# One level of Strassen's scheme in the second product of an attention and feed-forward kernel

## The chip, the cores and the metric

The kernel runs on one core of one Trainium2 chip. The metric is the device time of one execution in microseconds; the kernel before takes 854.92 us (median of three runs, 854.73 to 856.07). One further execution was taken by the hardware profiler, and every line of a profile below comes from such an execution. The engines are TensorE (PE in the profile; PEld is its loading of the stationary operand), VectorE (DVE), ScalarE (ACT), GpSimd (POOL) and SyncE (SP), which issues most of the DMAs.

## The reference

```python
# x: (8, 8, 512, 64)   state: (8, 8, 32, 64)   (batch, head, rows, D)
scores = x @ state.T / sqrt(D);  a  = softmax(scores);  xread = a  @ state
scores2 = state @ x.T / sqrt(D); a2 = softmax(scores2); sread = a2 @ x
attn = concatenate([xread, sread], axis=2)          # (8, 8, 544, 64)
t = attn.transpose(0, 2, 1, 3).reshape(8 * 544, 512)
h = t @ w_in                                         # w_in (512, 2048)
sp = maximum(h, 0) + log1p(exp(-abs(h)))             # softplus
g = h * erf(sp)
out = g @ w_out                                      # w_out (2048, 512)
```

x and state are f32. Both weights come as 64-bit floats, and the kernel turns them into f32 on the chip. All matmuls are f32.

## The kernel before, in words

There are nine chunks of rows: the 512 x rows of each of the eight batches, and one state chunk with the 8 × 32 = 256 state rows of all batches. Each chunk goes through a first product (rows by 512 times 512 by 2048), an elementwise step and a second product (rows by 2048 times 2048 by 512). The 2048 features are walked in four groups `g` of 512, so of four tiles of 128.

For a batch the first product is folded with the attention read: `mixed` (L229 to L232) multiplies the states with `w_in` into a tile `m`, two 128-row halves for each batch and group, and `hidden` multiplies that with the transposed softmax `aT`, so a tile of h needs two matmul calls. The state chunk takes its rows from `sT` and needs four calls a tile. `attention` (L126 and on) computes the softmax matrices of one batch: transposes into `xT` (L141, L143), scores (L151), softmax (L162 to L181), and in its inner function `rest` the second softmax and the read of x (L186 to L216). The weights are converted by `weight` (L100 to L104) group by group during batch 0.

`hidden` (L244 to L249) makes one group: four tiles `hp` in PSUM (a pool of two banks), each with a Softplus by ScalarE into `s` (L246) and a copy by VectorE into `hs` (L247); then one Erf by ScalarE over the whole of `s` (L248) and one multiplication by VectorE, `s = s * hs` (L249). `project` (L255) multiplies `s` as the stationary operand, 128 rows by 128 features at a time, with 512 columns of `w_out`, and adds up over all groups in one PSUM bank for each 128 rows, four accumulators `o0` to `o3`, with one buffer each. `store` copies them out by ScalarE (L263) and sends them off by SP's queue (L270 for batches, L277 for the state chunk).

The main loop is software-pipelined by one group: the code calls `hidden` of group g, and after it the projection of the group before (`pending`). After that come `mixed` of the next batch, one group in each turn, and once a batch `attention` of the next batch (in turn 3 of batch 0, in turn 1 of the others).

No queue is written out by hand. Inside its tile context the kernel gives each instruction a tile to read or write, and the framework's planner lays out the queue of each engine from the calls; an instruction that comes earlier in the code goes first where both are ready. The order in the trace is therefore not always the order of the calls. An engine then works through its own queue in that order, with semaphore waits on the others.

Of the kernel before, what the change touches and what calls it, by code (L numbers as in the profile page):

```python
# [8 lines left out]
F32 = mybir.dt.float32  # L9
U32 = mybir.dt.uint32  # L10
ALU = mybir.AluOpType
ACTF = mybir.ActivationFunctionType
# [4 lines left out]
def kernel(  # L17
# [23 lines left out]
    T = S + Ns  # L41
# [92 lines left out]
    def attention(b):  # L134
# [22 lines left out]
        a = att.tile([P, 2, NC * NI, Ns], F32, name="a")  # L157
# [25 lines left out]
        def rest():  # L183
            a2 = att.tile([P, 2, S], F32, name="a2")
# [50 lines left out]
    def hidden(pairs, n):  # L235

        hs = act.tile([P, GF, S], F32, name="hs")[:, :, 0:n]
        s = act.tile([P, GF, S], F32, name="s", bufs=3)[:, :, 0:n]  # L240
        for i in range(GF):
            hp = ps_h.tile([P, S], F32, name="h")
            for k, (lhsT, rhs) in enumerate(pairs):
                nc.tensor.matmul(out=hp[:, 0:n], lhsT=lhsT[:, P * i:P * i + P], rhs=rhs,  # L244
                                 start=(k == 0), stop=(k == len(pairs) - 1))
            nc.scalar.activation(out=s[:, i, :], in_=hp[:, 0:n], func=ACTF.Softplus)  # L246
            nc.vector.tensor_copy(hs[:, i, :], hp[:, 0:n])  # L247
        nc.scalar.activation(out=s, in_=s, func=ACTF.Erf)  # L248
        nc.vector.tensor_tensor(s, s, hs, op=ALU.mult)  # L249
        return s  # L250

    def project(gT, n, g, acc):
        for r in range(n // P):
            for i in range(GF):
                nc.tensor.matmul(out=acc[r], lhsT=gT[:, i, P * r:P * r + P],  # L255
                                 rhs=w_out[:, GF * g + i, :],
                                 start=(g == 0 and i == 0),
                                 stop=(g == NG - 1 and i == GF - 1))

    def store(acc, n, put):  # L260
        for r in range(n // P):
            ot = outs.tile([P, d_model], F32, name="ot")
            nc.scalar.copy(ot, acc[r])  # L263
            put(r, ot)

    def put_x(b):
        rows = out[T * b:T * b + S].rearrange("(p c) e -> c p e", c=NC)

        def go(r, ot):
            nc.sync.dma_start(out=rows[r], in_=ot)  # L270
        return go

    def put_s(r, ot):
        m = P // Ns
        for j in range(m):
            r0 = T * (m * r + j) + S
# [12 lines left out]
    pending = None  # L289
    for b, (n, put) in enumerate(chunks):  # L290
        acc = None
        for g in range(NG):
# [9 lines left out]
            gT = hidden(pairs(b, g), n)  # L302
# [47 lines left out]
```

## Time and profile before

| what | value |
|---|---|
| time, median of 3 runs | 854.92 us |
| time of the profiled execution | 856.09 us |
| span of the profiled execution, first to last instruction | 854.3 us |
| mean granted TensorE clock | 0.981 |
| busy TensorE, weight load, VectorE, ScalarE | 827.7, 379.0, 310.8, 388.9 us |
| matmul records of the second product (L255) | 1088 |

One call of `nc.tensor.matmul` on f32 operands appears as two matmul records and two weight-load records. In the views a group of instructions has its line, engine, operation, output and input with their shapes, the count after an x, then the busy time and the mean length of one in nanoseconds, and after a second bar the idle time of that engine just before them with what ended it. Busy times of TensorE are unions: records of neighbouring matmuls overlap, so the mean length of one is more than the spacing from one to the next. A row of the timeline or of the chain of waits has the start, the length, the engine, the line, the operation and how many were merged.

### The profile page before, as it was taken

How to read it: one execution, taken by the hardware profiler on the slowest of the kernel's cores; microseconds unless marked ns; L12 is line 12 of the kernel's file. 1: busy time of each engine (PE TensorE's matmuls, PEld its weight loads, DVE VectorE, ACT ScalarE, POOL GpSimd, SP SyncE). 2: the span in 40 equal slices, each digit the busy share in tenths (PEclk: the TensorE clock that was granted, in tenths of full speed). 3: DMA queues.
4: the chain of work that ended last, by engine and by line, in shares of the span. 5: the costliest groups of instructions: out<-in, count | busy, mean ns of one | idle time of the engine just before them, and what ended most of it. 6: DMA issues, size and time to landing. Idle time of an engine off the chain costs nothing.

```text
span 854.3 us, 7812 instructions
## 1 busy us (share of the span) xinstructions
PE 827.7 (97%) x3216; PEld 379.0 (44%) x3216; DVE 310.8 (36%) x436; ACT 388.9 (46%) x494; POOL 0.7 (0%) x6
## 2 busy tenths in 40 slices
PE   3689999999999999999999999999999999999997
PEld 2233345444444444454444444454444444445564
DVE  2979524452222522262224422262224322222121
ACT  5778535563344534373344534373445434333332
POOL 0000000000000000000000000000000000000000
PEclk7689999999999999999999999999999999999999
DMA  7658102002010200002010201000000001000100
GB/s 251 188 186 263 72 0 82 18 0 51 0 50 0 51 0 38 12 1 50 0 51 0 51 0 50 0 1 1 16 34 0 2 0 50 0 0 1 49 1 25
DMA packets 45474, 35.10 MB, mean 41 GB/s; under 512 B 36992, under 2 KB 36992, under 8 KB 45440
## 3 DMA queue, kind: packets, MB, share of 16 engines
q1 hardware_dynamic: 45056, 34.55, 13.1%
q8 instruction: 25, 0.41, 0.2%
q10 hardware_dynamic: 384, 0.07, 0.0%
q14 instruction: 9, 0.07, 0.0%
HBM read 25.69 MB, written 8.91 MB: 41 GB/s over the span
## 4 chain that ended last, share of the span: by engine, by line
PE 91%; DVE 0%; ACT 0%; issue 0%
PE o L255 53%; PE h L244 28%; PE at L229 4%; PE at L141 1%; PE at L151 1%; PE at L208 1%; PE at L196 1%; PE at L179 1%; PE at L162 1%; PE at L215 0%; PE at L130 0%; DVE m L232 0%; ACT ot L263 0%
## 5 line engine op out<-in xcount | busy, mean ns | idle before, releaser
L255 PE MATMUL o<-w_out,s 128*128 128x512 f32 x1088 | 484.2, 594 | 0.0
L255 PEld LDWEIGHTS o<-w_out,s 128*128 128x128 f32 x1088 | 203.8, 190 | 247.3 <-issue 244.6
L244 PE MATMUL h<-aT,m 128*128 128x512 f32 x512 | 241.8, 608 | 0.9 <-ACT m L231 0.7
L247 DVE COPY hs<-h 128x512 f32<-128x512 f32 (+1 forms) x144 | 94.9, 661 | 246.3 <-ACT s L246 246.2
L246 ACT ACTIVATE s<-h 128x512 f32<-128x512 f32 (+1 forms) x144 | 82.3, 573 | 185.5 <-PE h L244 185.0
L244 PEld LDWEIGHTS h<-aT,m 128*128 128x128 f32 x512 | 93.9, 193 | 125.8 <-issue 117.2
L249 DVE TENSOR_TENSOR s<-s,hs 128x2048 f32<-128x2048 f32 (+1 forms) x36 | 78.3, 2174 | 74.0 <-ACT s L248 74.0
L231 ACT COPY m<-at 128x512 f32<-128x512 f32 x32 | 18.7, 584 | 158.5 <-PE at L229 158.2
L232 DVE COPY m<-at 128x512 f32<-128x512 f32 x32 | 22.1, 690 | 169.7 <-PE at L229 169.7
L248 ACT ACTIVATE s<-s 128x2048 f32<-128x2048 f32 (+1 forms) x36 | 65.4, 1816 | 0.4
L246 ACT ACT_TABLE_LOAD x43 | 55.2, 1283 | 0.8
L263 ACT COPY ot<-o 128x512 f32<-128x512 f32 x34 | 19.7, 580 | 59.9 <-PE o L255 57.9
L248 ACT ACT_TABLE_LOAD x36 | 46.2, 1283 | 0.6
L229 PE MATMUL at<-w_in,stT 64*32 64x512 f32 x512 | 40.6, 628 | 0.4 <-DVE m L232 0.4
L244 PE MATMUL h<-sT,w_in 128*128 128x256 f32 x128 | 28.9, 379 | 0.0
L244 PEld LDWEIGHTS h<-sT,w_in 128*128 128x128 f32 x128 | 24.3, 190 | 6.7 <-issue 3.8
L143 ACT COPY xT<-at 128x512 f32<-128x512 f32 x32 | 17.3, 589 | 7.8 <-PE at L141 7.8
L141 PEld LDWEIGHTS at<-ident,x 128*128 128x128 f32 x128 | 15.9, 148 | 8.8 <-ACT m L231 3.5
L141 PE MATMUL at<-ident,x 128*128 128x128 f32 x128 | 17.9, 286 | 0.9 <-DMA x<-in_x_dram 0.9
L229 PEld LDWEIGHTS at<-w_in,stT 64*32 64x32 f32 x512 | 6.4, 106 | 27.0 <-issue 20.8
L179 PE MATMUL at<-ident,a 128*128 128x128 f32 x64 | 9.4, 292 | 7.7 <-DVE a L173 7.7
L151 PE MATMUL at<-xT,stT 64*32 64x512 f32 x128 | 11.9, 637 | 2.5 <-ACT xT L143 2.5
(50 smaller groups left out, 287.0 us busy)
## 6 DMA issues: line engine op xcount, KB each, us to landing
x<-in_x_dram SPq DMA_DIRECT2D x64, 128.0 KB, 3.3
raw<-in_moe_w_in_dram SPq DMA_DIRECT2D x8, 1024.0 KB, 5.9
hs<-in_moe_w_out_dram SPq DMA_DIRECT2D x8, 1024.0 KB, 5.2
out_dram<-ot SPq DMA_DIRECT2D x32, 256.0 KB, 2.3
out_dram<-ot SPq DMA_DIRECT2D x8, 64.0 KB, 1.7
st<-in_state_dram SPq DMA_DIRECT2D x8, 56.0 KB, 5.5
st<-in_state_dram ACTq DMA_DIRECT2D x8, 8.0 KB, 2.2
```

Source lines behind the costliest of these rows:

```text
L141: nc.tensor.transpose(out=xp[:, P * c:P * c + P], in_=xt[:, c, 2 * i:2 * i + 2, :], identity=ident)
L151: nc.tensor.matmul(out=s2[e][q, :], lhsT=stT[b][r, q], rhs=xT[r, i, :], start=True, stop=True)
L229: nc.tensor.matmul(out=ps[e][q, :], lhsT=stT[b][r, q], rhs=w_in[r, g, i, :], start=True, stop=True)
L231: nc.scalar.copy(mg[:, 0], ps[0])
L232: nc.vector.tensor_copy(mg[:, 1], ps[1])
L244: nc.tensor.matmul(out=hp[:, 0:n], lhsT=lhsT[:, P * i:P * i + P], rhs=rhs, start=(k == 0), stop=(k == len(pairs) - 1))
L246: nc.scalar.activation(out=s[:, i, :], in_=hp[:, 0:n], func=ACTF.Softplus)
L247: nc.vector.tensor_copy(hs[:, i, :], hp[:, 0:n])
L248: nc.scalar.activation(out=s, in_=s, func=ACTF.Erf)
L249: nc.vector.tensor_tensor(s, s, hs, op=ALU.mult)
L255: nc.tensor.matmul(out=acc[r], lhsT=gT[:, i, P * r:P * r + P], rhs=w_out[:, GF * g + i, :], start=(g == 0 and i == 0), stop=(g == NG - 1 a ...
L263: nc.scalar.copy(ot, acc[r])
```

## The change

The second product of batches 1 to 7 and of the state chunk goes by one level of Strassen's algorithm, in the variant with shared sums. It works on parts of 256 rows by 1024 features by 512 columns, each cut in two along all three: A11 to A22 are 128 rows by 512 features, B11 to B22 are 512 features by 256 columns. In place of eight products of such quarters there are seven. Batch 0 keeps the plain product.

The weight combinations T1, T2, T4 are made by three subtractions on VectorE at the end of batch 0 (`combine_w`); T3 overwrites B12 once batch 0's projection has read it (`last`). The combinations S1 to S4 of the activations are made for each part by `combine_g`, called at the head of `project7`, four VectorE operations of 128x512 that write over `hs`. `project7` adds up the seven products in seven half-banks of the four accumulators, over two parts of 1024 features. `store7` adds the half-banks together on VectorE, with one ScalarE copy, and puts out two times 128 rows.

A chunk's turns change with it: for batches 1 to 7 a turn is now 256 rows by 1024 features (two halves of rows, two parts of features each, in the order 0, 1, 1, 0), and the first product streams 256 columns in each matmul, two feature tiles side by side in one `hp` bank. The state chunk has two turns in place of four. `s` has two buffers in place of three, and the attention tiles `a` and `a2` become slices of a tile that takes the buffer of `xT`.

```diff
...
         for e in range(2):
             nc.scalar.copy(sc[:, e], s2[e])
-        a = att.tile([P, 2, NC * NI, Ns], F32, name="a")
+        both = att.tile([P, NI, S], F32, name="xT")
+        a = both[:, 0:2].rearrange("p e (k n) -> p e k n", n=Ns)
         aT[b] = keep.tile([P, 2, S], F32, name="aT")
...
             nc.vector.tensor_copy(aT[b][:, e], ps)
         def rest():
-            a2 = att.tile([P, 2, S], F32, name="a2")
+            a2 = both[:, 2:4]
...
-    def hidden(pairs, n):
-        hs = act.tile([P, GF, S], F32, name="hs")[:, :, 0:n]
-        s = act.tile([P, GF, S], F32, name="s", bufs=3)[:, :, 0:n]
-        for i in range(GF):
+    def hidden(b, fts, t0, n):
+        hs = act.tile([P, 4, S], F32, name="hs")
+        s = act.tile([P, 4, S], F32, name="s")
+        m = S // n
+        for i in range(4):
             hp = ps_h.tile([P, S], F32, name="h")
-            for k, (lhsT, rhs) in enumerate(pairs):
-                nc.tensor.matmul(out=hp[:, 0:n], lhsT=lhsT[:, P * i:P * i + P], rhs=rhs,
-                                 start=(k == 0), stop=(k == len(pairs) - 1))
-            nc.scalar.activation(out=s[:, i, :], in_=hp[:, 0:n], func=ACTF.Softplus)
-            nc.vector.tensor_copy(hs[:, i, :], hp[:, 0:n])
+            for j in range(m):
+                ops = pairs(b, fts[m * i + j], slice(t0, t0 + n))
+                for k, (lhsT, rhs) in enumerate(ops):
+                    nc.tensor.matmul(out=hp[:, n * j:n * j + n], lhsT=lhsT, rhs=rhs,
+                                     start=(k == 0), stop=(k == len(ops) - 1))
+            nc.scalar.activation(out=s[:, i, :], in_=hp, func=ACTF.Softplus)
+            nc.vector.tensor_copy(hs[:, i, :], hp)
         nc.scalar.activation(out=s, in_=s, func=ACTF.Erf)
         nc.vector.tensor_tensor(s, s, hs, op=ALU.mult)
-        return s
-    def project(gT, n, g, acc):
-        for r in range(n // P):
+        return s, hs
+    def project(gT, g, acc):
+        for r in range(NC):
             for i in range(GF):
                 nc.tensor.matmul(out=acc[r], lhsT=gT[:, i, P * r:P * r + P],
                                  rhs=w_out[:, GF * g + i, :],
                                  start=(g == 0 and i == 0),
                                  stop=(g == NG - 1 and i == GF - 1))
...
+    E2 = d_model // 2
+    wb = w_out.rearrange("p (g h i) (c e) -> p g h i c e", h=2, i=GF, c=2)
+    B11, B12, B21, B22 = (wb[:, :, h, :, c, :] for h in range(2) for c in range(2))
+    T = {}
+    def combine_w():
+        T[1], T[2] = (act.tile([P, 2 * GF * P * 2], U32, name="raw", bufs=2).bitcast(F32)
+                      .rearrange("p (g i e) -> p g i e", i=GF, e=E2) for _ in range(2))
+        T[4] = const.tile([P, NG // 2, GF, E2], F32, name="T4")
+        sub = lambda o, x, y: nc.vector.tensor_tensor(o, x, y, op=ALU.subtract)
+        sub(T[1], B12, B11)
+        sub(T[2], B22, T[1])
+        sub(T[4], B21, T[2])
+        def last():
+            sub(B12, B22, B12)
+            T[3] = B12
+        return last
+    def combine_g(gT, hs):
+        gv = gT.rearrange("p (h i2) (i1 r t) -> p h (i2 i1) r t", h=2, i1=2, r=2)
+        S4 = hs.rearrange("p (k i2) (i1 t) -> p k (i2 i1) t", i2=1, i1=GF)
+        A11, A12, A21, A22 = (gv[:, h, :, r, :] for r in range(2) for h in range(2))
+        S1, S2, S3, S4 = (S4[:, k] for k in range(4))
+        tt = nc.vector.tensor_tensor
+        tt(S1, A21, A22, op=ALU.add)
+        tt(S2, S1, A11, op=ALU.subtract)
+        tt(S3, A11, A21, op=ALU.subtract)
+        tt(S4, A12, S2, op=ALU.subtract)
+        return A11, A12, A22, S1, S2, S3, S4
+    def project7(gT, hs, g, first, last, acc):
+        A11, A12, A22, S1, S2, S3, S4 = combine_g(gT, hs)
+        for lhs, rhs, bank, c in ((A11, B11, 2, 0), (A12, B21, 0, 0), (A22, T[4], 1, 0),
+                                  (S2, T[2], 0, 1), (S3, T[3], 2, 1), (S1, T[1], 1, 1),
+                                  (S4, B22, 3, 0)):
+            for i in range(GF):
+                nc.tensor.matmul(out=acc[bank][:, E2 * c:E2 * c + E2], lhsT=lhs[:, i, :],
+                                 rhs=rhs[:, g, i, :], start=(first and i == 0 and c == 0),
+                                 stop=(last and i == GF - 1 and (c == 1 or bank == 3)))
+    def store7(acc, put):
+        twice = lambda t: t.unsqueeze(1).to_broadcast([P, 2, E2])
+        two = lambda t: t.rearrange("p (c e) -> p c e", c=2)
+        m1, u3 = (outs.tile([P, E2], F32, name=n) for n in ("m1", "u3"))
+        o1, o2 = (outs.tile([P, d_model], F32, name="ot") for _ in range(2))
+        c12 = o1[:, E2:]
+        add = lambda o, x, y: nc.vector.tensor_tensor(o, x, y, op=ALU.add)
+        nc.scalar.copy(m1, acc[2][:, 0:E2])
+        add(two(o1), twice(m1), two(acc[0]))
+        add(u3, c12, acc[2][:, E2:])
+        add(two(o2), twice(u3), two(acc[1]))
+        put(1, o2)
+        add(c12, c12, acc[1][:, E2:])
+        add(c12, c12, acc[3][:, 0:E2])
+        put(0, o1)
+    def put_x(b, h):
+        rows = out[TB * b:TB * b + S].rearrange("(p c) e -> c p e", c=NC)
         def go(r, ot):
-            nc.sync.dma_start(out=rows[r], in_=ot)
+            nc.sync.dma_start(out=rows[2 * h + r], in_=ot)
         return go
     def put_s(r, ot):
...
-    def pairs(b, g):
+    def pairs(b, f, toks):
+        g, fs = f // GF, slice(P * (f % GF), P * (f % GF) + P)
         if b < B:
-            mg = m_t.pop((b, g))
-            return [(mg[:, e], aT[b][:, e]) for e in range(2)]
-        return [(w_in[:, g, k, :], sT[:, k].rearrange("p b n -> p (b n)"))
+            return [(m_t[b, g][:, e, fs], aT[b][:, e, toks]) for e in range(2)]
+        return [(w_in[:, g, k, fs], sT[:, k].rearrange("p b n -> p (b n)")[:, toks])
                 for k in range(NK)]
+    def tiles(n):
+        return [ps_o.tile([P, d_model], F32, name="o%d" % r) for r in range(n)]
+    def plain(b):
+        box = []
+        def project_(g, gT):
+            if g == 0:
+                box.extend(tiles(NC))
+            project(gT, g, box)
+            if g == NG - 1:
+                store(box, lambda r, ot: put_x(b, r // 2)(r % 2, ot))
+        for g in range(NG):
+            yield lambda g=g: hidden(b, range(GF * g, GF * g + GF), 0, S)[0], \
+                lambda gT, g=g: project_(g, gT)
+    def fast(b, parts, put):
+        for h in range(parts):
+            box = []
+            def project_(gT, k, g, h, box):
+                if k == 0:
+                    box.extend(tiles(4))
+                project7(*gT, g, k == 0, k == 1, box)
+                if k == 1:
+                    store7(box, put(h))
+            for k in range(2):
+                g = k ^ (h & 1)
+                yield lambda g=g, h=h: hidden(b, range(2 * GF * g, 2 * GF * g + 2 * GF),
+                                              2 * P * h, 2 * P), \
+                    lambda gT, k=k, g=g, h=h, box=box: project_(gT, k, g, h, box)
     states(0)
     rest = attention(0)
-    chunks = [(S, put_x(b)) for b in range(B)] + [(B * Ns, put_s)]
-    pending = None
-    for b, (n, put) in enumerate(chunks):
-        acc = None
-        for g in range(NG):
+    pending = last = None
+    for b in range(B + 1):
+        if b == 0:
+            groups = plain(b)
+        elif b < B:
+            groups = fast(b, 2, lambda h, b=b: put_x(b, h))
+        else:
+            groups = fast(b, 1, lambda h: put_s)
+        for g, (first, second) in enumerate(groups):
             if b == 0:
                 weights_in(g)
                 mixed(0, g)
...
             if b + 1 < B and g == (1 if b == 0 else 0):
                 load_x(b + 1)
                 states(b + 1)
-            gT = hidden(pairs(b, g), n)
+            gT = first()
             if b == 0 and g == 0:
                 rest()
             if pending is not None:
                 pending()
-            if acc is None:
-                acc = [ps_o.tile([P, d_model], F32, name="o%d" % r) for r in range(n // P)]
-            def pending(gT=gT, n=n, g=g, acc=acc, put=put):
-                project(gT, n, g, acc)
-                if g == NG - 1:
-                    store(acc, n, put)
+            if last is not None:
+                last()
+                last = None
+            if b == 0 and g == NG - 1:
+                last = combine_w()
+            def pending(gT=gT, second=second):
+                second(gT)
             if b + 1 < B and (b or g):
                 for i in [g] if b or g > 1 else [0, 1]:
                     mixed(b + 1, i)
```

More of the change, by code (lines that the diff above doesn't have):

```diff
@@ L40 @@
     NG = NF // GF
-    T = S + Ns
+    TB = S + Ns
     scale = 1.0 / (D ** 0.5)
@@ L258, in project, with store @@
                                  stop=(g == NG - 1 and i == GF - 1))
-    def store(acc, n, put):
-        for r in range(n // P):
+    def store(acc, put):
+        for r in range(NC):
             ot = outs.tile([P, d_model], F32, name="ot")
@@ L264, in store @@
             put(r, ot)
-    def put_x(b):
-        rows = out[T * b:T * b + S].rearrange("(p c) e -> c p e", c=NC)
+    E2 = d_model // 2
[14 more added lines that the diff above has]
+        return last
@@ L275, in put_s @@
         for j in range(m):
-            r0 = T * (m * r + j) + S
+            r0 = TB * (m * r + j) + S
             nc.sync.dma_start(out=out[r0:r0 + Ns], in_=ot[Ns * j:Ns * j + Ns, :])
-    def pairs(b, g):
+    def pairs(b, f, toks):
+        g, fs = f // GF, slice(P * (f % GF), P * (f % GF) + P)
         if b < B:
-            mg = m_t.pop((b, g))
-            return [(mg[:, e], aT[b][:, e]) for e in range(2)]
-        return [(w_in[:, g, k, :], sT[:, k].rearrange("p b n -> p (b n)"))
+            return [(m_t[b, g][:, e, fs], aT[b][:, e, toks]) for e in range(2)]
+        return [(w_in[:, g, k, fs], sT[:, k].rearrange("p b n -> p (b n)")[:, toks])
```

## The prediction

> **What bounds the kernel now.** I read the page first: the busy times, then the chain that ended last.
>
> ```profile
> span 854.3 us, 7812 instructions
> PE 827.7 (97%) x3216; PEld 379.0 (44%) x3216; DVE 310.8 (36%) x436; ACT 388.9 (46%) x494; POOL 0.7 (0%) x6
> PE 91%; DVE 0%; ACT 0%; issue 0%
> ```
>
> TensorE's share is 97%, no other engine reaches half, and the chain is 91% TensorE. Next the busy time by stretches (columns: the stretch, its length, then busy time and instructions of PE, PEld, DVE, ACT, POOL, then the granted clock): does that hold where the second product runs?
>
> ```profile
> 0.00:50.00 50.00, 28.54 (x172) 13.14 (x173) 31.62 (x47) 33.39 (x42) 0.70 (x6) 0.73 0.68 200
> 200.00:400.00 200.00, 200.00 (x796) 88.83 (x795) 65.26 (x95) 86.60 (x113) 0.00 (x0) 1.00 0.09 25
> ```
>
> Only the opening has holes. From batch 1 on TensorE is busy all 200.00 us of a 200.00 us stretch, at clock 1.00. So the kernel is paid for in matmul streaming time, and less of it is less time, as long as no new wait appears. Which matmuls? The groups by line, shapes kept apart (one call of nc.tensor.matmul on f32 shows as two records):
>
> ```profile
> L255 PE MATMUL o<-w_out,s 128*128 128x512 f32 x1088 | 484.2, 594 | 0.0
> L244 PE MATMUL h<-aT,m 128*128 128x512 f32 x512 | 241.8, 608 | 0.9 <-ACT m L231 0.7 <-DVE hs L247 0.2
> L255 PEld LDWEIGHTS o<-w_out,s 128*128 128x128 f32 x1088 | 203.8, 190 | 247.3 <-issue 244.6 <-DVE s L249 0.7 <-ACT s L246 0.5
> L244 PEld LDWEIGHTS h<-sT,w_in 128*128 128x128 f32 x128 | 24.3, 190 | 6.7 <-issue 3.8
> ```
>
> The second product (L255) is 484.2 us, over half the span. Its mean of 594 ns is not its price, since neighbours overlap; the price is the spacing within a long run, which the chain of waits shows (columns: start, length, what):
>
> ```profile
> 345.60 1.72 PE o L255 x4
> 347.32 3.43 PE h L244 x8
> 350.75 12.02 PE o L255 x28
> 780.76 3.45 PE h L244 x16
> ```
>
> 28 records of 512 columns in 12.02 us are 0.4293 us each. The last row is the state chunk, whose first product has 256 columns: 16 in 3.45 us, 0.2156 us each. That is the price of the half-width matmul that the change is made of, measured in this kernel, each record with a weight load of its own (190 ns) that fits under 216.
>
> **The change part by part.** The columns streamed. The second product of batches 1 to 7 and of the state chunk is now 7 × 128 + 64 = 960 records of 512 columns: 960 × 0.4293 = 412.1 us. After, each 256 rows by 1024 features take seven products of four calls, 56 records of 256 columns; there are 7 × 2 × 2 + 2 = 30 such steps, so 1680 × 0.2156 = 362.2 us. That is −49.9 us. Batch 0 stays plain. The first product of batches 1 to 7 is split into 256 columns: 7 × 64 = 448 records at 0.4293 (192.3 us) become 896 at 0.2156 (193.2 us), +0.9. On TensorE the sum is −49.0 us.
>
> The first place where a rule speaks against it. Weight loads grow by 720 + 448 = 1168, and at 190 ns they sit 88% full under each 0.2156 us matmul. In the state chunk 16 of them in a row did not lengthen the spacing, so I charge nothing. The Trainium skill, "TensorE: Matmul & The Clock Gate", Part 3, The mechanism, says that a weight load overlaps a running matmul only where its row group differs, and these all use the full array; by that rule each added load would stand in the open. The spacing of 0.2156 us with loads of 190 ns beneath it contradicts that here.
>
> The combinations on VectorE, four adds of 128x512 a step. The rows for the prices:
>
> ```profile
> L173 DVE TENSOR_TENSOR a<-a,z 128x512 f32<-128x512 f32 x16 | 10.3, 682 | 0.0
> L249 DVE TENSOR_TENSOR s<-s,hs 128x2048 f32<-128x2048 f32 x32 | 73.4, 2293 | 66.2 <-ACT s L248 66.2
> L247 DVE COPY hs<-h 128x256 f32<-128x256 f32 x16 | 6.8, 425 | 46.4 <-ACT s L246 46.4
> ```
>
> Four at 0.682 are 2.7 us a step, 82 us in all. They need only the finished product s × hs of their own step (L249). Where can they lie? One step of batch 3, VectorE's timeline (start, length; in brackets the idle time before):
>
> ```profile
> 351.42 0.69 DVE L247 COPY hs<-h 128x512 f32<-128x512 f32 x1 [1.02 <-ACT s L246]
> 354.64 2.29 DVE L249 TENSOR_TENSOR s<-s,hs 128x2048 f32<-128x2048 f32 x1 [2.53 <-ACT s L248]
> 363.92 0.69 DVE L232 COPY m<-at 128x512 f32<-128x512 f32 x1 [6.99 <-PE at L229]
> ```
>
> After the product VectorE is idle for 6.99 us, and 2.7 fit there. The first product of this step ends on TensorE at 347.32 + 3.43 = 350.75, s is final at 354.64 + 2.29 = 356.93, so the four sums are there at 359.7. The step's own second product starts only after the projection of the step before it: 56 records less the 8 already used as filler (the o x4 between the h runs, at half width) are 48 × 0.2156 = 10.3 us, so it starts at 361.1 or later, and its first three operands are not sums at all. If the sums are queued there they cost nothing. But the code calls them after the next step's `hidden`, so this rests on the planner queueing them by readiness and not in the order of the code. The first batch shows that it does so on VectorE:
>
> ```profile
> 45.84 0.47 DVE L213 TENSOR_SCALAR sn<-at,z 128x64 f32<-128x64 f32 x2
> 47.63 2.29 DVE L249 TENSOR_TENSOR s<-s,hs 128x2048 f32<-128x2048 f32 x1 [1.31 <-ACT s L248]
> ```
>
> L213 belongs to `rest()`, which the code calls after the first `hidden`, and yet it runs ahead of that hidden's last instruction, L249. How far ahead can it reach? The chain in an attention window:
>
> ```profile
> 280.38 4.29 PE o L255 x10
> 289.86 1.03 PE at L208 x64
> ```
>
> The ten projection records are called after the rest of attention and after a whole further `hidden`, and run before attention's L208: a reach like the one that the sums need.
>
> The waits that this adds, and who stands behind them. Each step's sums wait for L249; queued behind them are only the copy of `mixed` (L232) and the next hidden copies, 7 us later. `store7` puts on VectorE, per 256 rows, two adds of 512 (0.682) and three of 256 (0.425): 2.6 us, instead of ScalarE copies. They wait for the last products, and the bank copies of the next step (L247) are queued behind them. The last add can follow the last matmul by about 0.4 us, while the first h bank of the next step is full only after its 1.72 us of matmuls and its Softplus: free. The next 256 rows reuse the four accumulators; the first product goes to bank 2, which is read out two products (3.4 us) before the end: free in the plan.
>
> Weight combinations, once: three subtractions of 128x2048 at 2.29 before batch 1, 6.9 us, and one, T3, after batch 0's projection has read B12. VectorE there:
>
> ```profile
> 104.46 1.22 DVE L104 SCALAR_TENSOR_TENSOR w_out<-hs,w_out 128x1024 uint32<-128x1024 uint32 x1
> 113.25 0.69 DVE L247 COPY hs<-h 128x512 f32<-128x512 f32 x1 [1.03 <-ACT s L246]
> 116.48 2.29 DVE L249 TENSOR_TENSOR s<-s,hs 128x2048 f32<-128x2048 f32 x1 [2.53 <-ACT s L248]
> 124.04 0.69 DVE L232 COPY m<-at 128x512 f32<-128x512 f32 x1 [5.27 <-PE at L229]
> ```
>
> w_out is complete at 105.7, and the idle times in these rows are 5.27 behind the product and 2.53 before it, with attention's VectorE part after 124. Between 0 and 6.9 us; I take 1.0, near the low end, since TensorE has batch 0's projection to run meanwhile. T3 is needed at the fifth product of batch 1's first step, after two hidden calls: 0, at most 2.3.
>
> Attention windows (batches 2 to 7, six of them): an add or a product queued ahead of a link of attention's chain delays it, by 0.68 us, or by 2.29 where two or three adds stand together. TensorE has the projection as filler meanwhile (the o x10 above), so the cost lies between 0 and 6 × 2.3 = 14 us; I take 1.5, near the end that the filler speaks for. s goes from three buffers to two, and a, a2 move into xT's tile; in program order each earlier reader is done before the new writer can be ready, as the projection two steps back ends before a third hidden begins: 0, and if that fails, one fill of 1.72 us (the o x4 above) in each window. The end: today a copy of 0.58 us follows the last matmul, then a 0.425 add:
>
> ```profile
> 836.71 12.89 PE o L255 x30
> 849.62 0.58 ACT ot L263
> ```
>
> −0.2 us. The output DMAs stay the same in number and size on SP's queue, two at each 256 rows in place of four at each 512.
>
> Sum: −49.0 + 1.0 + 1.5 − 0.2 = −46.7. The profiled execution took 856.09 us (span 854.3 and 1.79 around it): 809.4. The median of the runs, 854.92, lies 1.17 below that execution: 808.2, say **808.5 us**. By the bounds: 854.92 − 49.2 = 805.7 with everything hidden, 854.92 − 49.0 + 6.9 + 2.3 + 14 = 829 with every ceiling paid.
>
> **The rivals.** First, accumulators that come late. If the read-out of store7 is not through when the next step's filler wants bank 2, the filler o x4 (1.72 us) turns into idle time at each of the 14 borders between 256-row parts: 14 × 1.72 = 24 us, about 832. For it: one buffer per accumulator, and a bank shared by two products. Against it: only the last of five adds needs the last product.
>
> Second, the other side: the sums queued as the code has them, behind the next step's product L249. Then VectorE is held by ScalarE's chain for them:
>
> ```profile
> DVE s L249 <- ACT s L248: 74.0, 36, 2.5
> ```
>
> From the end of hidden (350.75) to the end of L249 (356.93) are 6.18 us, and S1 and S2 add 2 × 0.682: 7.54. TensorE has only three products without sums, 24 × 0.2156 = 5.17 us, and 8 records of them are already spent as filler: 3.45 left. It would stall 4.1 us in each step outside the attention windows, 29 − 6 = 23: +94, about 902 us, slower than before. It decides from 12 steps on: 12 × 4.1 = 49 eats the gain. Against it stand the rows of L213 and of the o x10. The Trainium skill, "TensorE: Matmul & The Clock Gate", Architectural detail, says that VectorE's queue is strict first-in first-out, so whatever order the planner wrote is kept however wrong its clock was; no row here shows VectorE passing a waiting instruction, and with that rule the rival hangs wholly on the planner.
>
> Third, that only about 12 steps are so queued: gain and stall cancel, 855.
>
> Fourth, the loads of the first place in the open: 1168 × 0.19 = 222 us more, about 1030; the 0.2156 us row is against it.
>
> **How the numbers follow.** Forecast 0.77; late accumulators 0.12; sums behind L249 0.08 with the fourth at 0.01 beside it; cancelled 0.02. Measurement cannot tell less than 0.2% (1.7 us) from no change. Faster: 0.77 + 0.12 = 0.89; same 0.02; slower 0.09. The range takes the forecast's bounds and the milder part of late accumulators: 804.5 to 826; 829 needs every ceiling at once and is left out.
>
> **What would show it.** Right: about 1808 o records, L255's successor at 0.2156 in long runs, each batch 6.5 us shorter; the combination adds directly behind L249 with the idle time before the L232 copy down from 7 to about 4 us; TensorE still busy 200 of 200. Wrong: idle TensorE released by VectorE sums (second rival), by store7's adds (first), or matmul runs spaced wider than 0.22 us with weight loads end to end (fourth).

## The result, and the profile after

The changed kernel takes 817.79 us (median of four runs, 817.07 to 818.49), against 854.84 us before; the ratio is 0.956 with a 95% interval of 0.955 to 0.958. The forecast was 808.5 us in a range of 804.5 to 826. So 37 us were gained and not 46: the time is in the range and the sign is right, but some 9 us of the gain are missing. The profiled execution took 817.85 us, its span is 816.1 us. Its page:

```profile
span 816.1 us, 10344 instructions
PE 784.9 (96%) x4384; PEld 598.3 (73%) x4384; DVE 429.0 (53%) x625; ACT 370.4 (45%) x465; POOL 0.7 (0%) x6
PE 88%; ACT 5%; DVE 3%; DMA 3%; issue 1%; SPq 0%
```

TensorE is still the bound, with 1168 more records and 43 us less busy time. VectorE took on 118 us and weight loads 219 us, and neither became the bound. New in the chain are small shares of ScalarE, VectorE and DMA. By stretches (same columns as before):

```profile
200.00:400.00 200.00, 199.51 (x1190) 162.69 (x1189) 103.67 (x160) 88.15 (x113) 0.00 (x0) 1.00 0.10 29
```

199.51 of 200: there are holes now, but they are 0.49 us. By this column little of what is missing is idle time; but the ends of TensorE's records are modelled, and the starts of the rows will show below that more is lost around the holes. The price of a half-width record, from the two longest runs of the chain, and the length of a batch, from the start of the first product in turn 3 of batches 2 and 3 (after, then before):

```profile
294.49 3.65 PE h L253 x16
383.55 3.65 PE h L253 x16
...
773.29 13.81 PE h L253 x64
787.10 24.19 PE o L317 x112
```

```profile
298.22 3.63 PE h L244 x8
392.75 3.63 PE h L244 x8
```

112 records in 24.19 us are 0.2160 us each and 64 in 13.81 are 0.2158, where the forecast had 0.2156. A batch went from 392.75 − 298.22 = 94.53 to 383.55 − 294.49 = 89.06 us: 5.47 less, where the forecast's streaming gives 6.53. VectorE in one step (before, 6.99 us lay idle ahead of the copy of mixed):

```profile
327.10 2.29 DVE L258 TENSOR_TENSOR s<-s,hs 128x2048 f32<-128x2048 f32 x1 [2.53 <-ACT s L257]
329.43 0.69 DVE L303 TENSOR_TENSOR hs<-s 128x512 f32<-128x512 f32 x1
...
331.84 0.68 DVE L306 TENSOR_TENSOR hs<-s,hs 128x512 f32<-128x512 f32 x1
...
335.16 0.69 DVE L238 COPY m<-at 128x512 f32<-128x512 f32 x1 [0.67 <-PE at L235]
```

The four sums (L303 to L306) stand right behind their product, in the gap that was named for them; in this step adds of `store7` lie between and behind them.

Where the time went can be read from landmarks on TensorE: the last transpose of each `rest` (before at 46.46, 143.64, 197.25 and, the eighth, 669.91; after at 47.09, 145.89, 198.53 and 644.10), the first matmul of the state chunk (780.60; 747.22) and the end of the span. The forecast column is streaming alone at 0.4293 and 0.2156 us a record, by the records in the stretch.

| stretch | before, us | after, us | forecast | measured |
|---|---|---|---|---|
| start to first rest | 46.5 | 47.1 | 0 | +0.6 |
| first to second rest (batch 0) | 97.2 | 98.8 | −0.4 | +1.6 |
| second to third rest | 53.6 | 52.6 | −3.3 | −1.0 |
| third to eighth rest (five batches) | 472.7 | 445.6 | −32.6 | −27.1 |
| eighth rest to the state chunk | 110.7 | 103.1 | −7.7 | −7.6 |
| state chunk to the end | 73.7 | 68.8 | −5.0 | −4.8 |

The last two stretches, which have no attention, keep their forecast to 0.2 us. The shortfall is in batch 0 and wherever attention runs.

### The profile page after: what moved, and what is told of

It is laid out like the page before. It is cut to its first block, busy times and chain, and to the rows that moved or that the text cites. A ratio compares the mean times of both kernels' runs of the same rounds, so it can differ in the third digit from the quotient of the medians.

```text
span 816.1 us, 10344 instructions
## 1 busy us (share of the span) xinstructions
PE 784.9 (96%) x4384; PEld 598.3 (73%) x4384; DVE 429.0 (53%) x625; ACT 370.4 (45%) x465; POOL 0.7 (0%) x6
## 4 chain that ended last, share of the span: by engine, by line
PE 88%; ACT 5%; DVE 3%; DMA 3%; issue 1%; SPq 0%
PE o L317 44%; PE h L253 30%; PE at L235 4%; PE o L264 4%; DMA hs<-in_moe_w_out_dram 1%; PE at L168 1%; PE at L146 1%; PE at L185 1%; ACT L255 1%; PE at L202 1%; PE at L214 1%; DMA raw<-in_moe_w_in_dram 1%; ACT s L255 1%; DVE s L258 1%; ACT s L257 0%
## 5 line engine op out<-in xcount | busy, mean ns | idle before, releaser
L253 PE MATMUL h<-aT,m 128*128 128x256 f32 (+1 forms) x960 | 243.4, 401 | 1.9 <-ACT m L237 1.8
L253 PEld LDWEIGHTS h<-aT,m 128*128 128x128 f32 x960 | 178.8, 191 | 67.2 <-issue 33.7
L256 DVE COPY hs<-h 128x512 f32<-128x512 f32 x136 | 93.4, 690 | 198.2 <-ACT s L255 198.2
L255 ACT ACTIVATE s<-h 128x512 f32<-128x512 f32 x136 | 80.3, 597 | 170.9 <-PE h L253 170.5
L258 DVE TENSOR_TENSOR s<-s,hs 128x2048 f32<-128x2048 f32 x34 | 77.9, 2292 | 77.1 <-ACT s L257 77.1
L317 PE MATMUL o<-raw,hs 128*128 128x256 f32 x480 | 115.7, 380 | 0.0
L317 PE MATMUL o<-w_out,s 128*128 128x256 f32 x480 | 115.0, 379 | 0.0
L317 PE MATMUL o<-w_out,hs 128*128 128x256 f32 x480 | 113.4, 379 | 0.0
L317 PEld LDWEIGHTS o<-w_out,hs 128*128 128x128 f32 x480 | 91.2, 190 | 12.4
L317 PEld LDWEIGHTS o<-w_out,s 128*128 128x128 f32 x480 | 90.2, 190 | 12.6 <-DVE s L258 0.8
L317 PEld LDWEIGHTS o<-raw,hs 128*128 128x128 f32 x480 | 90.2, 190 | 12.3
L264 PE MATMUL o<-w_out,s 128*128 128x512 f32 x128 | 58.8, 598 | 0.0
L317 PE MATMUL o<-T,s 128*128 128x256 f32 x240 | 56.7, 379 | 0.0
L255 ACT ACT_TABLE_LOAD x41 | 52.6, 1283 | 0.7
L317 PEld LDWEIGHTS o<-T,s 128*128 128x128 f32 x240 | 45.1, 190 | 5.9
L264 PEld LDWEIGHTS o<-w_out,s 128*128 128x128 f32 x128 | 23.4, 190 | 30.4 <-issue 30.3
L235 PE MATMUL at<-w_in,stT 64*32 64x512 f32 x512 | 41.6, 630 | 0.9 <-ACT m L237 0.5
```

Source lines behind the costliest of these rows:

```text
L235: nc.tensor.matmul(out=ps[e][q, :], lhsT=stT[b][r, q], rhs=w_in[r, g, i, :], start=True, stop=True)
L253: nc.tensor.matmul(out=hp[:, n * j:n * j + n], lhsT=lhsT, rhs=rhs, start=(k == 0), stop=(k == len(ops) - 1))
L255: nc.scalar.activation(out=s[:, i, :], in_=hp, func=ACTF.Softplus)
L256: nc.vector.tensor_copy(hs[:, i, :], hp)
L317: nc.tensor.matmul(out=acc[bank][:, E2 * c:E2 * c + E2], lhsT=lhs[:, i, :], rhs=rhs[:, g, i, :], start=(first and i == 0 and c == 0), stop ...
```

## The experiments

Two theories of that shortfall were tested. Theory A: VectorE's new work stands in attention's and batch 0's way. Theory B: the half-width structure itself changes the order that the planner writes into the queues, and the sums are free.

**No sums** (`no_sums`). The four sums are left out, and plain quarters of A stand in their place; the matmuls stay the same in number and shape.

```diff
-        tt(S1, A21, A22, op=ALU.add)
-        tt(S2, S1, A11, op=ALU.subtract)
-        tt(S3, A11, A21, op=ALU.subtract)
-        tt(S4, A12, S2, op=ALU.subtract)
-        return A11, A12, A22, S1, S2, S3, S4
+        return A11, A12, A22, A21, A22, A21, A12
```

> The changed kernel with the four activation sums S1 to S4 left out (plain quarters of A stand in their place, so that part of the computation is changed); the seven products and everything else stay. Two theories on the 10.7 us by which the span fell short of the 49.0 us of saved TensorE streaming. Theory A: VectorE's new work stands in the way of attention's chain and of batch 0; without the 82 us of sums most of the loss in the six attention windows goes, 811 to 814 us. Theory B: the loss comes from how the queues are re-cut around half-width turns, and the sums are free as forecast; 816.5 to 819 us.

817.89 us (815.93 to 819.19), ratio 0.956, interval 0.954 to 0.958: no difference from the changed kernel. The batch is the same to 0.01 us (381.64 − 292.58 = 89.06):

```profile
292.58 3.65 PE h L253 x16
...
381.64 3.65 PE h L253 x16
```

The 82 us of sums cost nothing, in attention's windows too. Theory A falls for the sums.

**No weight subtractions** (`no_wsub`). All four are left out, and plain quarters of B stand in their place.

```diff
-        sub(T[1], B12, B11)
-        sub(T[2], B22, T[1])
-        sub(T[4], B21, T[2])
+        T[1], T[2], T[4] = B12, B22, B21
...
-            sub(B12, B22, B12)
             T[3] = B12
```

> The changed kernel with the four weight subtractions left out (T1 to T4 are plain quarters of B, so that part of the computation is changed). Theory A: the subtractions stand in front of batch 0's last weight conversion and of one copy of the mixed tile on VectorE, which delays the last w_out transfer by 3.5 us; without them batch 0 ends 2 to 3 us earlier, 815 to 816 us. Theory B: the start varies by itself, and the time stays at 817.8 within 0.8.

816.65 us (814.10 to 817.19), ratio 0.954, interval 0.952 to 0.955. By time alone 1.1 us is at the limit of what can be told. The profile is plainer: from first to second rest it takes 144.70 − 47.57 = 97.13 us, the 97.18 of before and not the 98.80. The rows of VectorE show what the subtractions pushed. The changed kernel first, then the one without them:

```profile
84.52 2.29 DVE L286 TENSOR_TENSOR raw<-w_out 128x2048 f32<-128x2048 f32 x1
...
96.79 2.29 DVE L258 TENSOR_TENSOR s<-s,hs 128x2048 f32<-128x2048 f32 x1 [2.53 <-ACT s L257]
99.00 1.22 DVE L108 CUSTOM_DVE_ANT_0 w_out<-hs,w_out 128x2048 uint16<-128x2048 uint16 x1
```

```profile
94.09 1.23 DVE L108 CUSTOM_DVE_ANT_0 w_out<-hs,w_out 128x2048 uint16<-128x2048 uint16 x1 [0.34 <-ACT hs L106]
...
97.32 2.29 DVE L258 TENSOR_TENSOR s<-s,hs 128x2048 f32<-128x2048 f32 x1 [0.73 <-ACT s L257]
```

With T1's subtraction (L286) in the queue, a weight conversion (L108) is planned behind the product L258 and not ahead of it, 4.9 us later. It frees the buffer into which the last piece of w_out is loaded, so that transfer is issued at 99.5 us and not at 97.0. Behind it stand that piece's conversions on ScalarE and then a copy of `mixed`, for which TensorE waits in the changed kernel:

```profile
106.57 3.70 PE L253 MATMUL h<-aT,m 128*128 128x512 f32 x8 [1.11 <-ACT m L237]
```

A second wait, 0.48 us at 127.85 behind T3's subtraction, is shown in the last section. Together they are 1.59 us, and the kernel without subtractions has neither.

**Eight products in the new structure** (`eight`): the turns, half-width matmuls and buffers of the changed kernel, without sums and subtractions, and with two ScalarE copies in place of `store7`'s adds. The diff shows the products alone.

```diff
-        A11, A12, A22, S1, S2, S3, S4 = combine_g(gT, hs)
-        for lhs, rhs, bank, c in ((A11, B11, 2, 0), (A12, B21, 0, 0), (A22, T[4], 1, 0),
-                                  (S2, T[2], 0, 1), (S3, T[3], 2, 1), (S1, T[1], 1, 1),
-                                  (S4, B22, 3, 0)):
+        for lhs, rhs, bank, c, f, e in (
+                (A11, B11, 2, 0, 1, 0), (A12, B21, 2, 0, 0, 0),
+                (A11, B12, 2, 1, 0, 0), (A12, B22, 2, 1, 0, 1),
+                (A21, B11, 0, 0, 1, 0), (A22, B21, 0, 0, 0, 0),
+                (A21, B12, 0, 1, 0, 0), (A22, B22, 0, 1, 0, 1)):
```

> The changed kernel's turns, half-width matmuls, buffers and order of batches, but the plain eight products of quarters in place of seven, without sums and weight subtractions; two ScalarE copies store each part. By the columns alone it streams 30 x 8 = 240 matmul records of 256 columns more than the changed kernel, 51.7 us. If the structure (theory B) holds the loss, 817.8 + 51.7 = 869.5 us, within 2. If the sums and subtractions hold it (theory A), the structure is free and it comes out at 854.8 + 2.7 = 857.5 to 861. If weight loads came into the open with twice as many half-width matmuls, over 900.

865.59 us (865.06 to 867.40), ratio 1.011, interval 1.010 to 1.013. The time lies between the two that were expected, 869.5 and 857.5 to 861, nearer the first. The structure alone is slower than the kernel before by 10 us, of which streaming at the forecast's prices explains 2.7; 7 us are its own. A batch takes 302.95 − 206.99 = 95.96 us:

```profile
206.99 3.65 PE h L253 x16
...
302.95 3.65 PE h L253 x16
```

Per batch that is 95.96 − 89.06 = 6.90 above the changed kernel, for 32 records more: 32 × 0.2160 = 6.91. So the eighth product is worth just its streaming. Against the kernel before, 1.43 a batch more less 0.37 of streaming leaves 1.06, just as in the changed kernel (6.53 − 5.47). Weight loads in the open would have brought it over 900; they are excluded.

**Sums behind the next turn's product** (`sums_behind`), the rival of the other sign:

```diff
-        A11, A12, A22, S1, S2, S3, S4 = combine_g(gT, hs)
+        with tc.issue_after(getattr(mult[-1], 'ins', mult[-1])):
+            A11, A12, A22, S1, S2, S3, S4 = combine_g(gT, hs)
```

> The changed kernel with the sums of each part queued on VectorE behind the product s * hs of the next turn, as the code calls them, by an ordering edge without a wait. The rival of the prediction prices it at 4.1 us in each of 23 turns: 817.8 + 94 = 912 us, with TensorE idle before the product with S2, released by VectorE. If the place in the queue does not matter, 818.

838.21 us (one run, against 855.64 before): 20 us slower than the changed kernel, not 94, and still faster than before. The place in the queue does matter, at a fifth of the price. Its VectorE and then its TensorE around one step:

```profile
331.90 2.29 DVE L260 TENSOR_TENSOR s<-s,hs 128x2048 f32<-128x2048 f32 x1 [2.53 <-ACT s L259]
334.11 0.68 DVE L305 TENSOR_TENSOR hs<-s 128x512 f32<-128x512 f32 x1
```

```profile
330.01 1.89 PE L320 MATMUL o<-T,s 128*128 128x256 f32 x8
331.83 1.09 PE L235 MATMUL at<-w_in,stT 64*32 64x512 f32 x16
332.85 1.56 PE L255 MATMUL h<-aT,m 128*128 128x256 f32 x6
334.85 0.70 PE L320 MATMUL o<-raw,hs 128*128 128x256 f32 x2 [0.44 <-DVE hs L305]
```

After the three products without sums (the last is the row of L320 with T) the planner fills the hole with `mixed` (L235) and six records of the following turn's first product, and TensorE waits 0.44 us and not 4.1. The view of waits has 9.6 us for TensorE's wait on these sums, in 17 waits; the rest of the 20 us is not taken apart here.

**Half-width first product in the kernel before** (`half_first`):

```diff
-            for k, (lhsT, rhs) in enumerate(pairs):
-                nc.tensor.matmul(out=hp[:, 0:n], lhsT=lhsT[:, P * i:P * i + P], rhs=rhs,
-                                 start=(k == 0), stop=(k == len(pairs) - 1))
+            for c in range(0, n, S // 2):
+                for k, (lhsT, rhs) in enumerate(pairs):
+                    nc.tensor.matmul(out=hp[:, c:c + S // 2], lhsT=lhsT[:, P * i:P * i + P],
+                                     rhs=rhs[:, c:c + S // 2],
+                                     start=(k == 0), stop=(k == len(pairs) - 1))
```

> The kernel before with one edit: each 512-column call of the first product is two calls of 256 columns. The loss of the changed kernel that stays when sums and subtractions are gone is 1.06 us in each batch. If half-width records of the first product, as filler in attention's window, bring it by another cut of the queues, the batch period goes from 94.53 to 95.5 or more (0.13 of it streaming), 7 us in all. If it belongs to the turns of 256 rows, to s with two buffers or to a and a2 in xT's tile, the period is 94.7 and the time about 1 us above before.

863.52 us (one run, against 855.87). One edit, no Strassen, and a batch goes to 302.33 − 206.96 = 95.37 us:

```profile
206.96 3.65 PE h L245 x16
...
302.33 3.65 PE h L245 x16
```

That is 0.84 above before, 0.13 of it forecast as streaming, against the 1.06 in question. The 95.5 asked for was missed by 0.13, but the other branch said 94.7; most of the structural loss belongs to the half-width first product. Where it sits: the chain of waits in an attention window, before and after (transposes L141/L146, scores L151/L156, transposes of the scores L162/L168):

```profile
272.92 1.72 PE h L244 x4
274.64 1.24 PE at L151 x16
275.87 1.06 PE h L244 x2
276.93 0.87 PE at L162 x8
```

```profile
268.55 0.47 PE at L146 x4
...
269.04 0.51 ACT xT L148
...
270.13 1.28 ACT L255
...
271.43 0.60 ACT s L255
272.02 0.49 ACT sc L160
...
272.56 1.15 PE at L168 x8
```

Before, TensorE carries the chain. After, with finer filler, attention's transposes stand closer together, all four copies of xT are done before ScalarE's table load and Softplus (L255), these two come in ahead of the copy of the scores, and the chain goes over ScalarE until TensorE stands idle ahead of L168 for 0.24 us. TensorE's timeline, after and then before:

```profile
271.19 1.13 PE L253 MATMUL h<-aT,m 128*128 128x256 f32 x4
272.56 1.15 PE L168 MATMUL at<-ident,sc 128*128 128x128 f32 x8 [0.24 <-ACT sc L160]
273.54 2.76 PE L253 MATMUL h<-aT,m 128*128 128x256 f32 x12
```

```profile
275.80 1.13 PE L244 MATMUL h<-aT,m 128*128 128x512 f32 x2
276.77 1.04 PE L162 MATMUL at<-ident,sc 128*128 128x128 f32 x8
277.64 2.74 PE L244 MATMUL h<-aT,m 128*128 128x512 f32 x6
```

Reckoned by starts the place costs more than its idle time. From the filler to the transposes are 1.37 us after and 0.97 before, for the same columns, and from the transposes to the next filler 0.98 and 0.87: 0.51 us lost. In the same way, the transposes of x (L146) lose 0.08 us in this window and those of a and a2 (L185, L202) 0.24. That makes 0.83 of the 1.06; the record price is 0.13 more. The kernel with a half-width first product has the first two as well, 0.51 (its wait is again 0.24 us, released by ScalarE's copy of the scores) and 0.08, but not the third.

**Score copies on VectorE** (`sc_dve`), to take that link away:

```diff
-            nc.scalar.copy(sc[:, e], s2[e])
+            nc.vector.tensor_copy(sc[:, e], s2[e])
```

> The changed kernel with one edit: the two score copies of attention (sc) go from ScalarE to VectorE. In its attention windows TensorE waits 0.24 us for those copies, which stand on ScalarE behind a table load and a Softplus. If that queue place is the structural loss, the batch period falls from 89.06 to between 88.0 and 88.7 and the time by 3 to 7 us, 811 to 815. If the loss is the cost of switching between tile shapes and more pieces, the period stays within 0.2 of 89.06 and the time at 817 to 818.

818.75 us (815.74 to 819.93), ratio 0.956, interval 0.953 to 0.958: no gain. The wait ahead of L168 is gone, and the batch still takes 88.95 us (from one rest to the next), 0.11 less. Its TensorE at that place:

```profile
273.53 0.60 PE L168 MATMUL at<-ident,sc 128*128 128x128 f32 x4
273.97 0.60 PE L253 MATMUL h<-aT,m 128*128 128x256 f32 x2
274.40 0.60 PE L168 MATMUL at<-ident,sc 128*128 128x128 f32 x4
```

The transposes now come in two pieces between pairs of half-width records, and lose nothing here. But further on the read of x (L214), which ran in one piece of 64 records, is cut into two of 32, and by the starts of the rows most of the 0.5 us comes back there and at the transposes beside it. Taking one late link away moved the loss and did not end it. In batch 0 the copies also stand among weight conversions: the first rest ends at 52.6 us and not 47.1.

**Attention one turn later** (`turn2`):

```diff
-                if g == (NG - 1 if b == 0 else 1):
+                if g == (NG - 1 if b == 0 else 2):
```

> The changed kernel with the next batch's attention called one turn later (turn 2, where the first product of features 1024 to 2047 is the filler behind it). If the structural 0.86 us in each batch hang on where the links of attention's chain fall between the half-width records, the batch period moves from 89.06, either way by 0.2 to 1 us; if they are a fixed price of switching shapes, it stays within 0.1.

817.28 us (one run), the batch 89.06 us as before the edit. The loss does not hang on the turn: the wait ahead of L168 is there again, 0.24 us.

**Subtractions later** (`wsub_late`, `late_sc`, `wsub_late_again`, `late_sc_from2`, `after_again`). The subtractions are queued behind the last VectorE instruction of the first batch's attention, alone and with the score copies on VectorE for all batches or from batch 2 on.

```diff
-            if b == 0 and g == NG - 1:
-                last = combine_w()
...
                     attention(b + 1)()
+            if b == 0 and g == NG - 1:
+                with tc.issue_after(sn_op[-1]):
+                    last = combine_w()
...
-            nc.scalar.copy(sc[:, e], s2[e])
+            (nc.vector.tensor_copy if b > 1 else nc.scalar.copy)(sc[:, e], s2[e])
```

> The changed kernel with the weight subtractions queued on VectorE behind the first batch's attention, still before their first use. The kernel without subtractions had the batch-0 stretch, from the end of one rest to the next, at 97.13 in place of 98.80. If their place in front of batch 0's conversions costs that, this one has it at 97.1 to 97.4 and comes out 1.2 to 1.7 us faster, near 816.3. If they cost wherever they stand, 817.8 as before.

> Both edits together, a candidate for the fastest version: subtractions behind the first attention, and the score copies on VectorE. If both causes hold and add, 810 to 814 us; if only the first holds, 816.3; if the longer VectorE queue in batch 0 eats it, 818 or more.

> The changed kernel as it is, for a comparison on one chip with the next two: 817 to 818.5 us, ratio to before about 0.956.

> The changed kernel with the weight subtractions behind the first batch's attention, once more, now beside the changed kernel on one chip. From the stretch from the end of the first rest to the end of the third (150.55 us against 151.44 in the profiles) 0.9 us less, and up to 1.6 by the medians of the first measurement: 816.2 to 817. If the start's own variation made that difference, no difference.

> The same, and the score copies on VectorE for batches 2 to 7 only. On VectorE for all batches they cost 5.9 us in the first attention, where VectorE is full of weight conversions, and gave back 2.5 us between the end of the third rest and the last matmul (609.85 us against 612.4). Without the first loss: 1.8 us below the run before it, 814 to 815.5. If the two do not separate, 816 to 818.

| kernel | median, us | ratio to before | interval |
|---|---|---|---|
| wsub_late | 816.26 | 0.9535 | 0.9521 to 0.9549 |
| late_sc | 819.16 | 0.9567 | 0.9547 to 0.9587 |
| after_again | 817.34 | 0.9548 | 0.9529 to 0.9567 |
| wsub_late_again | 816.00 | 0.9538 | 0.9520 to 0.9556 |
| late_sc_from2 | 816.37 | 0.9539 | 0.9524 to 0.9553 |

The last three ran on one chip. Late subtractions came out faster both times, 1.5 us against the first measurement of the changed kernel and 1.3 beside it on one chip, but the intervals overlap, so no version is shown to beat the changed kernel. Part of what the batch-0 stretch gains (143.29 − 46.49 = 96.8 us in place of 98.8) the next one gives back (54.4 in place of 52.6). There, in `wsub_late_again`, the four subtractions stand on VectorE from 142.86 to 153.69 us, among the copies of batch 1's first product, and TensorE then waits 1.59 us, at 160.31, for s × hs. So the subtractions cost in both places that were tried. The candidate with the score copies missed its 814 to 815.5.

## Why the prediction was right, and where it was short

**TensorE is the bound and the product count decides.** Right, and shown by the eighth product: taken back, it costs 6.90 us a batch where its records stream for 6.91.

**The price of a half-width record.** Right in kind, 0.2160 in place of 0.2156 us. On 2576 records that is 0.9 us of the missing 9, hardly more than the rounding of the row it was read from: 3.45 us over 16 records is known to 0.0003 us a record.

**Weight loads free.** Right. 112 records in a row keep 0.2160 us with a load each, and the loads are busy for 73% of the span. The rule of the Trainium skill, "TensorE: Matmul & The Clock Gate", Part 3, The mechanism, that loads overlap only where the row group differs, does not hold for these runs; the same section also has a load run ahead where it goes to a background weight buffer, and these runs do not contradict that.

**Sums free, planner by readiness.** Right on both counts: the rows of L303 to L306 stand in the named gap, and the kernel without them takes as long. The rival that puts them behind the next product had the right sign against the changed kernel and a price 4.6 times too high (20 us measured): its step "It would stall 4.1 us in each step" left out that the planner would draw `mixed` and the following turn's first product into the hole, as the one step shown has it.

**`store7` and the accumulators.** The first rival, late accumulators at 24 us, did not come: in the steps without attention the filler is there (o L317 x6 between the runs of h) and the stretch from the eighth rest to the state chunk keeps the forecast to 0.2 us.

**Batch 0.** "I take 1.0" for the subtractions, and 0 for T3: the stretch grew by 1.6 where streaming alone would have taken 0.4 off, and 1.67 go when the subtractions are left out. T3 is the 0.48 us in which TensorE waits behind it, so 0 was too low. The other 1.11 us did not come the way that was named: T1 did not fill VectorE's idle time, it changed the planned order so that a conversion, and with it the last transfer of w_out, came later. A wait of that kind is not the subtractions' alone: `half_first`, which has none, waits 1.20 us for the copy of `mixed` at 105.78. The start up to the first rest varied from 45.4 to 47.6 us between runs of kernels that do not differ there, so the 0.6 us in the table is no effect of the change.

**Attention windows.** This is the step that failed, in its size and in the engine that it named. It read "an add or a product queued ahead of a link of attention's chain delays it", with 1.5 us in all. The streaming column is missed by 5.5 us between the third and the eighth rest and by 2.3 between the second and the third, 7.8 us in all, 0.7 of it the record price. The sums bring none of it (no difference without them), nor do the adds of `store7` (the kernel with eight products has neither and loses the same 1.06 us a batch). What stands ahead of a link is ScalarE's table load and Softplus, ahead of the copies of the scores: 0.51 us in the window shown, with 0.32 at the other transposes. So a queue place ahead of a link does delay it, but on ScalarE and not on VectorE, and one edit, the half-width first product, brings 0.59 of it into the kernel before. The forecast charged that split with 0.9 us of streaming and did not ask what finer filler does to the order of attention's links. That attention's windows could cost up to 14 us was in its bounds; the 826 that ends its range was set for late accumulators, which did not come.

Between the second and the third rest, one more thing is new. TensorE's timeline after the change:

```profile
159.06 1.04 PE L235 MATMUL at<-w_in,stT 64*32 64x512 f32 x2
...
176.03 1.08 PE L235 MATMUL at<-w_in,stT 64*32 64x512 f32 x14
```

The 16 records of one `mixed`, which before stand together and take 1.09 us, are cut in two, and the piece of two takes nearly as long as the whole. With 0.83 us at the transposes that explains most of the 2.3.

A rival, a fixed price of switching shapes, is not the cause: from the fourth rest to the fifth TensorE changes shape 25 times before and 27 times after, and the changes between 64*32 and 128*128 tiles, which do cost time, are as many in both. What stays open is some 0.1 us in each window, and which of the other edits (turns of 256 rows, half-width second product, fewer buffers) brings the 0.24 us at L185 and L202.

By the terms: price 0.9; windows 7.8 less the 0.7 of price counted there and the 1.5 allowed, 5.6; batch 0 and the start 2.6, so 1.6 beyond the 1.0 taken; the 0.2 that the end was to gain, and did not: together 8.3 of the 8.5 us between the forecast span (854.3 − 46.7 = 807.6) and 816.1.

## What to carry to other kernels

Where one engine is busy 200 us of 200, taking away its work is worth its measured spacing, and a shape that already runs somewhere in the trace gives that spacing before the change is built. Combinations on another engine are free as long as the planner can put them into a gap that the trace shows; check the gap's length and how far the planner reaches. The price of such a change lies in what is cut finer beside it: cost the stretches where TensorE alternates with short dependent work by themselves, since there a split that streams for almost nothing still cost 0.7 us a batch on its own, and 1.06 with the rest of the structure. And look for such a cost in the starts of the rows: the idle time shown was half of what one late link cost.

## What the runs showed of the hardware

Behind the 64*32 matmuls of `mixed`, the first records on 128*128 tiles take longer, in both profiles. In the chain of an attention window after the change:

```profile
265.16 1.02 PE at L235 x16
266.18 1.06 PE h L253 x4
```

Four half-width records stream for 4 × 0.2160 = 0.86 us, but take 1.06 here by their modelled ends, and 0.96 by the starts of the timeline's rows (266.11 to 267.07). Before, the same place has 1.05 for two full ones (0.86), and 0.96 by starts. Transposes and streaming records, both on 128*128 tiles, follow each other at no such price where their inputs are there: in the kernel before, eight transposes and two full records take turns in 0.87 and 0.86 us.

VectorE did not pass a waiting instruction. T3's subtraction waits for the third group of batch 0's projection, and the copy of mixed behind it waits with it, until TensorE waits for the copy (VectorE, then TensorE):

```profile
124.90 2.29 DVE L286 TENSOR_TENSOR w_out<-w_out 128x2048 f32<-128x2048 f32 x1 [3.30 <-PE o L264]
127.11 0.68 DVE L238 COPY m<-at 128x512 f32<-128x512 f32 x1
```

```profile
124.79 1.09 PE L235 MATMUL at<-w_in,stT 64*32 64x512 f32 x16
127.85 0.66 PE L146 MATMUL at<-ident,x 128*128 128x128 f32 x4 [0.48 <-DVE m L238]
```

The matmuls of mixed end at 125.88, the copy starts at 127.11. The Trainium skill, "TensorE: Matmul & The Clock Gate", Architectural detail, calls VectorE's queue strict first-in first-out; these rows agree.
